# A block-recurrent attention and a mixture-of-depths layer on one core: another way out for the score rows, wider reads, and a new order

## The chip, the cores and the metric

The kernel runs on one core of a Trainium2 chip. The metric is the device time of one execution in microseconds. The core has five engines: PE (TensorE: matrix products and transposes, into PSUM), DVE (VectorE), ACT (ScalarE), POOL (GpSimd) and SP (SyncE, here only a queue that issues DMAs), and 16 DMA engines that all queues share.

## The reference, cut to what matters

```python
B, H, S, Ns, D = 8, 8, 512, 32, 64       # x: (B,H,S,D)   state: (B,H,Ns,D)
scores  = scale * x @ state^T;  a  = softmax(scores);   xread = a  @ state    # (B,H,S,D)
scores2 = scale * state @ x^T;  a2 = softmax(scores2);  sread = a2 @ x        # (B,H,Ns,D)
y = concat([xread, sread], axis=2)       # to (B, 544, 512): row s, column h*64 + d
scores = y @ w_gate                      # (B, 544)
for b in range(B):
    top = argpartition(-scores[b], 128)[:128]
    h   = maximum(y[b, top] @ w1, 0)     # w1: 512 x 1024
    out[b, top] = y[b, top] + sigmoid(scores[b, top]) * (h @ w2)   # w2: 1024 x 512; the other rows: out = y
```

All in float32.

## The kernel before, in words

The work is cut into some 690 named pieces, each on one engine. `add(name, engine, fn, after, takes, uses)` records a piece; `carry_out` then emits them in the sequence of the string `ORDER`, which is written out by hand: each engine runs its own pieces in that sequence and waits where it must. In a word such as `first3.4@6`, 3 is the batch, 4 a part of it, and 6 the PSUM bank that the piece takes; `~5@0` are five transposes of the identity that nobody uses. Eight batches overlap in this order. Per batch b:

- `ldx` loads x[b] (1 MB). `turn` transposes it on PE, four 128x128 transposes to a piece (L393), and `turned` copies the result out of PSUM on ACT (L402). For the batches in `ON_DVE` a second load `ldy` brings x in blocks, in 128-byte runs (L318), and `blocks` transposes 32x32 blocks on DVE (L382).
- `scores` (L418) gives both score matrices, heads four to a group g. `smax`, `sexp`, `ssum` are the softmax over the sequence; `xmax`, `xspread`, `xsub`, `xexp` are that over the state (batches 0 and 1 in halves).
- `read b.r` (L506) reads the state for half r of the rows. A head's 32 state rows lie on 32 partitions, four heads q beside each other; 16 matmuls of 32 x 128 by 66 columns: 64 of the state, one of gates (state times `w_gate`), one of ones. `zsum` inverts the sums, `gate` makes the row scores `sc[:, b, 2r:2r+2]`, `rows` scales the output rows (on ACT for chunks 1 and 3, else on DVE), `stx` stores them.
- `turna`/`turneda` transposes the second softmax on PE and ACT; for the batches in `A_BLOCKS`, `ablocks` turns blocks on DVE, and `aout` and four `ain` take them through DRAM (L544, L548). `sread` (L579) reads x, `srows` scales, `sts` stores.
- `sgate`, `heads`, `sscore`: gate of the state rows. A product with `w_gate` summed per partition, a matmul that adds up the heads, a copy of that column into `sc[:, b, 4]`.
- The scores must lie along the free dimension on all partitions (`srow`, 544 wide). Batches 0 to 3: `row b.r` and `srow` transpose the score columns on PE, `rowk` and `srowk` copy on ACT. Batches in `ROW_DMA`: `rowout` (four columns) and `srowout` (the state's) write them to DRAM element by element, `rowin` reads the row back broadcast to 128 partitions.
- `win` compares each score with all later ones, `over` adds up on PE, `off` and `oh` make a one-hot matrix of the chosen rows, `pick` on PE gives their numbers and scores. `fetch` (POOL, L611) gathers the 128 chosen rows from the stored output, so it waits for `stx` and `sts` too; `below`, `exps`, `sigmoid` make the gate.
- `xg` transposes the gathered rows (L770, copy `xgk`), `first b.0` to `first b.7` are the first layer (L792, eight records of 128 columns each), `relu` (L795), `second b.k.f0` the second (L814), `add` adds, `put` (POOL) scatters the rows.

A float32 matmul stands in the trace as two records. SP issues nearly all DMAs in the sequence of the order, so a DMA whose issue is held up holds up those behind it.

Of the kernel before, what the change touches and what calls it, by code (L numbers as in the profile page):

```python
# [8 lines left out]
F32 = mybir.dt.float32  # L9
# [22 lines left out]
    first0.0@1 sigmoid0 smax3 srowk1 xexp2 first0.1 ldw2.1 win1.0 sexp3.0 first0.2 xmax3 sexp3.1 first0.3 sexp2.1 xspread3
    first0.4@7 relu0.0 first0.5 ssum3 xsub3 turna2.1@6 first0.6 turneda2.1 ssum2 xexp3 ablocks3.0 read2.0@0 ablocks3.1 win1.1 aout3
    sread2@6 win1.2 stturn4@5 win1.3 srows2 ldy5.0 first0.7 win1.4 stkept4 sts2 sgate2 zsum2.0 over1@4 rows2.0 relu0.4 heads2
    second0.0.0@5 ain3.0 gate2.0 rows2.1 sscore2 off1 oh1 blocks4.0 second0.0.2 blocks4.1 ldy5.3 blocks4.2 ldy5.1 pick1 second0.0.4
    picked1 index1 below1 blocks4.3 fetch1 exps1 sigmoid1 read2.1@0 ldy5.2 second0.0.6 zsum2.1 rows2.2 rows2.3 gate2.1 ain3.1
    parts2 srow2 row2.0@7 add0.0 row2.1 rowk2 scores4.0@4 put0.0 srowk2 scores4.1 win2.0 stx2 xg1@7 smax4 read3.0@0 xgk1 blocks5.0
    sexp4.0 first1.0@7 zsum3.0 rows3.0 sexp4.1 first1.1 ain3.2 ablocks4.0 rows3.1 first1.2 ablocks4.1 first1.3 gate3.0 aout4 ssum4
    win2.1 row3.0@6 relu1.0 read3.1@0 win2.2 win2.3 first1.4@7 ain3.3 zsum3.1 gate3.1 rows3.3 rows3.2 first1.5 ain4.0 xmax4
    first1.6 xspread4 first1.7 stx3 sread3@3 relu1.4 xsub4 ain4.1 second1.0.0@7 xexp4 win2.4 ldx6.0 blocks5.1 ldx6.1 blocks5.2  # L40
    srows3 scores5.0@4 sts3 sgate3 blocks5.3 over2@2 scores5.1 off2 oh2 ain4.2 heads3 row3.1 pick2 smax5 second1.0.2 rowk3 index2
    sexp5.0 sscore3 fetch2 picked2 xmax5 second1.0.4 sexp5.1 ablocks5.0 below2 parts3 exps2 sigmoid2 second1.0.6 ain4.3 ablocks5.1
    ssum5 aout5 xspread5 srow3 xg2@6 srowk3 add1.0 read4.0@0 xgk2 xsub5 put1.0 sread4@7 zsum4.0 xexp5 ain5.0 gate4.0 first2.0@6
    rows4.0 ldy6.0 srows4 win3.0 first2.1 rows4.1 sgate4 first2.2 win3.1 sts4 win3.2 first2.3 ain5.1 win3.3 read4.1@0 win3.4
    relu2.0 ldx7.0 ldx7.1 over3@6 zsum4.1 heads4 gate4.1 rows4.3 first2.4@5 ldy6.1 sscore4 off3 parts4 oh3 first2.5 rows4.2
    first2.6 ain5.2 first2.7 second2.0.0@7 relu2.4 rowout4 pick3 read5.0@0 picked3 index3 ldy6.2 below3 fetch3 exps3 sigmoid3
    second2.0.2 ldy6.3 zsum5.0 rows5.0 gate5.0 rows5.1 second2.0.4 srowout4 ain5.3 second2.0.6 stx4 xg3@6 add2.0 rowin4 read5.1@0
# [12 lines left out]
    exps6 sigmoid6 second5.0.2 srows7 sts7 sgate7 heads7 second5.0.4 sscore7 parts7 srowout7 xg6@7 second5.0.6 rowin7 xgk6 add5.0  # L60
    first6.0@7 put5.0 first6.1 win7.0 first6.2 win7.1 first6.3 win7.2 win7.3 first6.4@6 relu6.0 win7.4 over7@7 first6.5 off7 oh7
# [8 lines left out]
def kernel(  # L70
# [10 lines left out]
    nc = tc.nc  # L81
# [172 lines left out]
    def pool_tables():  # L254
# [10 lines left out]
        for over in overs:  # L265
            nc.gpsimd.memset(over, 0.0)
# [621 lines left out]
```

## Time and profile before

| | |
|---|---|
| median of 3 runs (lowest, highest) | 251.94 us (251.03, 254.04) |
| the profiled execution | 251.55 us |
| its span, first to last instruction | 249.8 us |
| mean granted TensorE clock | 0.917 of full |
| busy: PE, weight loads, DVE, ACT, POOL | 202.0, 153.1, 121.2, 86.7, 34.8 us |
| DMA | 37.20 MB in 74945 packets, 61480 of them under 512 B |
| chain that ended last, by engine | DMA 32%, PE 26%, DVE 14%, ACT 10%, SP queue 8%, issue 7% |

Busy times are shares of one execution and add up over engines that work at the same time. The span is what the instructions take; the time of an execution is 1.75 us longer. The granted clock has two levels here, 1.00 for 2.4 GHz and 0.50 for 1.2.

### The profile page before, as it was taken

To read this page: it belongs to the slowest core of one execution; us is meant where nothing else is said; L and a number is where in the kernel's file an instruction comes from. 1 tells how busy PE (TensorE), PEld (TensorE's weight loads), DVE (VectorE), ACT (ScalarE), POOL (GpSimd) and SP (SyncE) were. 2 spreads that over 40 slices of the span, in tenths; PEclk is the share of its full clock that TensorE was granted. 3 is DMA by queue.
4 is the path that set the end of the run, shared out by engine and by line. 5 is a ranking of instruction groups with operands and counts; after the bars stand their busy time and mean duration, and the time that the engine had idled before them with its cause. 6 is when DMAs were issued, how large, how long until landed. Compare 5 with 4: busy or idle time off the path is not lost.

```text
span 249.8 us, 5630 instructions
## 1 busy us (share of the span) xinstructions
PE 202.0 (81%) x2305; PEld 153.1 (61%) x2305; DVE 121.2 (49%) x335; ACT 86.7 (35%) x257; POOL 34.8 (14%) x99
## 2 busy tenths in 40 slices
PE   7967896899799989992699959949249829889991
PEld 6646674795489439950579438925039624765981
DVE  3685686898386988331429507496104300240000
ACT  3675694865364236430033202072103101010000
POOL 8000203000220031121001201003100021120112
PEclk9997999999999999997569977999956968999999
DMA  7999989958965988799699592908429450600101
GB/s 211 330 339 356 253 275 207 251 201 149 173 210 151 285 181 146 211 82 69 132 220 80 117 169 106 129 2 269 27 76 106 40 175 11 89 10 31 45 0 42
DMA packets 74945, 37.20 MB, mean 149 GB/s; under 512 B 61480, under 2 KB 69672, under 8 KB 73896
## 3 DMA queue, kind: packets, MB, share of 16 engines
q1 hardware_dynamic: 72824, 32.26, 63.4%
q0 software_dynamic: 1296, 4.20, 7.2%
q8 instruction: 18, 0.29, 0.6%
q10 hardware_dynamic: 800, 0.39, 0.6%
q14 instruction: 7, 0.06, 0.1%
HBM read 23.20 MB, written 13.64 MB: 148 GB/s over the span
## 4 chain that ended last, share of the span: by engine, by line
DMA 32%; PE 26%; DVE 14%; ACT 10%; SPq 8%; issue 7%; POOLq 0%; POOL 0%; ACTq 0%; DVEq 0%
DMA xr<-out_dram,idx 12%; PE banks L792 7%; PE banks L814 6%; SPq L318 6%; ACT xs L524 6%; DMA xf<-in_x_dram 5%; DMA aT<-a_d 5%; PE banks L506 4%; DMA s_d<-sc 4%; DMA srow<-s_d 4%; PE banks L579 3%; DVE xs L526 2%; DVE nm L465 2%; PE banks L770 2%; DVE eT L456 2%
## 5 line engine op out<-in xcount | busy, mean ns | idle before, releaser
L792 PE MATMUL banks<-xg,w 128*128 128x128 f32 x512 | 65.9, 289 | 0.0
L792 PEld LDWEIGHTS banks<-xg,w 128*128 128x128 f32 x512 | 62.9, 203 | 2.7 <-issue 1.6
L814 PE MATMUL banks<-w,hT 128*128 128x512 f32 (+1 forms) x144 | 59.9, 559 | 3.2 <-ACT hT L795 3.2
L814 PEld LDWEIGHTS banks<-w,hT 128*128 128x128 f32 x144 | 26.3, 193 | 23.8 <-issue 19.4
L524 ACT ACTIVATE xs<-banks,rz 128x64 f32<-128x64 f32 x128 | 28.0, 332 | 22.6 <-DVE xs L526 12.2
L671 DVE SCALAR_TENSOR_TENSOR win<-srow,sc,after 128x544 bf16<-128x544 f32 (+4 forms) x40 | 18.3, 504 | 9.8 <-DMA srow<-s_d 9.2
L770 PE MATMUL banks<-ident,xr 128*128 128x128 f32 x32 | 6.4, 334 | 19.2 <-DMA xr<-out_dram,idx 19.2
L506 PEld LDWEIGHTS banks<-st_v,eT 32*128 32x128 f32 x512 | 19.2, 213 | 4.3 <-issue 3.2
L506 PE MATMUL banks<-st_v,eT 32*128 32x66 f32 x512 | 21.6, 305 | 0.2 <-ACT eT L460 0.2
L795 ACT ACTIVATE hT<-banks 128x512 f32<-128x512 f32 x16 | 9.7, 605 | 31.5 <-PE banks L792 31.1
L817 DVE SCALAR_TENSOR_TENSOR ot<-banks,z,xr 128x512 f32<-128x512 f32 (+1 forms) x9 | 6.1, 680 | 28.4 <-PE banks L814 28.4
L770 PEld LDWEIGHTS banks<-ident,xr 128*128 128x128 f32 x32 | 4.5, 170 | 23.6 <-issue 13.2
L382 DVE STREAM_TRANSPOSE xT<-xf 128x512 f32<-128x512 f32 x16 | 10.5, 688 | 17.4 <-DMA xf<-in_x_dram 17.4
L773 ACT COPY xg<-banks 128x512 f32<-128x512 f32 x8 | 4.7, 591 | 37.6 <-PE banks L770 37.6
L579 PE MATMUL banks<-xf,aT 128*32 128x64 f32 x512 | 11.3, 255 | 5.9 <-DMA aT<-a_d 5.5
L469 ACT ACTIVATE a<-banks,nm 128x512 f32<-128x512 f32 x16 | 11.1, 694 | 13.9 <-DVE nm L465 8.8
L579 PEld LDWEIGHTS banks<-xf,aT 128*32 128x32 f32 x512 | 9.8, 133 | 7.0 <-issue 6.5
L183 PE MATMUL banks<-ident 128*128 128x128 f32 x37 | 7.2, 346 | 7.8 <-ACT xs L524 3.2
L611 POOL DMA_INDIRECT xr<-out_dram,idx x8 | 8.4, 1047 | 34.3 <-DVE z L725 25.4
L526 DVE TENSOR_TENSOR xs<-banks,rz 128x512 f32<-128x512 f32 x16 | 10.9, 684 | 4.5 <-ACT xs L524 4.3
L418 PE MATMUL banks<-xT,st_T 64*32 64x256 f32 x256 | 12.2, 410 | 0.6 <-DVE eT L456 0.4
L611 POOL DMA_INDIRECT out_dram<-ot,idx x7 | 7.6, 1079 | 36.4 <-DVE ot L817 35.8
(87 smaller groups left out, 209.8 us busy)
## 6 DMA issues: line engine op xcount, KB each, us to landing
out_dram<-xs SPq DMA_DIRECT2D x8, 1024.0 KB
xf<-in_x_dram SPq DMA_DIRECT2D x14, 512.0 KB
xf<-in_x_dram SPq DMA_DIRECT2D x19, 256.0 KB
w<-in_moe_w_dram SPq DMA_DIRECT2D x4, 1024.0 KB
a_d<-a_b SPq DMA_DIRECT2D x5, 512.0 KB
aT<-a_d SPq DMA_DIRECT2D x20, 128.0 KB
srow<-s_d SPq DMA_DIRECT2D x4, 272.0 KB
out_dram<-xt SPq DMA_DIRECT2D x16, 32.0 KB
```

Of the source, the lines that this page charges most:

```text
L318: nc.sync.dma_start(out=view_x2(b)[o:o + 32], in_=src)
L418: nc.tensor.matmul(view_s()[Ns * q:Ns * (q + 1), w, g], st_T[half, b, g, Ns * q:Ns * (q + 1)], xT[2 * g + q // 2].ap[half, q % 2].rearrang ...
L469: nc.scalar.activation(out=a.ap[:, g], in_=view_s()[:, :, g], func=AF.Exp, bias=tmp["nm"][:, g:g + 1], accum_out=tmp["ss"][:, g:g + 1])
L506: nc.tensor.matmul(view(o)[:, q, w, g], eT.ap[k, w, g, r], st_v[k, b, g], start=True, stop=True)
L524: nc.scalar.activation(out=to[:, q, g], in_=view(o)[:, q, w, g, 0:D], func=AF.Copy, scale=rz[:, q, g:g + 1])
L526: nc.vector.tensor_tensor(out=to, in0=view(o)[:, :, w, :, 0:D], in1=rz.unsqueeze(3).to_broadcast([128, 4, 2, D]), op=ALU.mult)
L579: nc.tensor.matmul(o2.ap[k, D * g:D * (g + 1)], aT.ap[:, g, c, k], view_x(b)[:, 4 * g + q, c], start=(c == 0), stop=(c == NC - 1))
L611: touches(b, nc.gpsimd.indirect_dma_start(**kw), True)
L671: nc.vector.scalar_tensor_tensor(wins[c][0:n, 0:SP - f], srow.ap[0:n, f:SP], sc[0:n, b, c:c + 1], after[0:n, 0:SP - f], op0=ALU.is_gt, op1 ...
L770: nc.tensor.transpose(v[:, j, 0:m], u["xr"].ap[0:m, 128 * j:128 * (j + 1)], ident[0:m, 0:m])
L792: nc.tensor.matmul(o, w(j), i[:, :, j] if n == 256 else i[:, 0, j], start=(j == 0), stop=(j == ND - 1))
L814: nc.tensor.matmul(py.ap[0:m, 0:part.stop - part.start], hT.ap[:, f, lo:lo + m], w2[:, f, part], start=(f == 0), stop=(f == NF - 1))
```

## The change

- **Score rows through DRAM.** `sc` gets 32 columns per batch, zeroed at the start by POOL. A new DVE piece `rowblk` transposes its 32x32 blocks, so that each partition holds 32 scores in a row, and one DMA `rowout` writes 128 runs of 128 bytes, zero columns too (16 KB). `rowout`'s wait now includes the state's score; `srowout` is gone. `ROW_DMA` becomes batches 3 to 7.
- **Sums over heads.** `heads` multiplies the broadcast partial sums with `same_n`, 32 columns wide, which leaves the state's score row on all partitions at once; `srowk` copies it from there, `srow` is gone, and `sscore` takes the diagonal.
- **Wider reads.** For batches 1, 3, 5, 7 (`READ64`), POOL builds `st_2` (pieces `beside`): for each pair of heads the state of one in columns 0 to 65, of the other in 66 to 131, zeros elsewhere. A read is then 8 matmuls of 64 x 128 by 132 columns; `rows` on DVE takes two instructions instead of one. In all batches a PSUM bank now holds another part of the read.
- **Who turns what.** `ON_DVE` is 6 and 7 (was 4 to 7), `A_BLOCKS` 4 to 7 (was 3 to 7).
- **The order** is a new one. Ahead of `first0.0` now stand all turns of batches 0 to 5, the scores of 0 to 3, the state reads of 0 to 3 and the reads of x for 0, 1 and the first half of 2. Two stretches of it:

```text
(PE, from second2.0.0 to xg4)
second2.0.0@6 read4.0@0 over3@7 second2.0.2 pick3 second2.0.4 read4.1@0 second2.0.6 scores6.0@4 scores6.1 xg3@7 read5.0@0
first3.0@7 ... first3.7 read5.1@0 over4@7 second3.0.0@6 pick4 second3.0.2 sread5@7 scores7.0@4 scores7.1 read6.0@0 heads5
second3.0.4 xg4@7
(SP, in the same part)
ldy7.0 sts4 aout5 ldy7.3 ldy7.2 ain5.0 ldy7.1 ain5.1 rowout4 stx4 rowin4 ain5.2 aout6 ain5.3 ain6.0 ain6.1 stx5 ain6.2
```

```diff
-    ON_DVE = (4, 5, 6, 7) if planned else ()
-    A_BLOCKS = (3, 4, 5, 6, 7) if planned else ()
+    ON_DVE = (6,7)
+    A_BLOCKS = (4,5,6,7)
+    READ64 = (1,3,5,7)
-    ROW_DMA = (4, 5, 6, 7) if planned else ()
+    ROW_DMA = (3,4,5,6,7)
...
-    R_SD = Ring("s_d", [1, SP], 2, F32, dram)
+    R_SD = Ring("s_d", [32 * 128], 2, F32, dram)
+    R_SB = Ring("s_b", [128, 32], 2)
...
-    same_n = const.tile([128, 128], F32, name="same_n")
-    sc = const.tile([128, B, NC + 1], F32, name="sc")
+    same_n = const.tile([128, Ns], F32, name="same_n")
+    sc = const.tile([128, B, 32], F32, name="sc")
+    st_2 = const.tile([128, max(len(READ64), 1), 2, 2 * DV], F32, name="st_2")
...
+    def beside(b):
+        for q in range(4):
+            k, o = slice(Ns * q, Ns * (q + 1)), DV * (q % 2)
+            nc.gpsimd.tensor_copy(out=st_2[k, READ64.index(b), :, o:o + DV], in_=st_v[k, b])
+
+    for b in READ64:
+        p_bd[b] = add(f"beside{b}", "POOL", lambda b=b: beside(b), after=[p_sg[b], p_tab])
...
+                def read(r=r, o=o):
+                    for w in range(2):
+                        for g in range(2):
+                            for u in range(2):
+                                k = slice(2 * Ns * u, 2 * Ns * (u + 1))
+                                nc.tensor.matmul(view(o)[:, w, u, 2 * g:2 * g + 2].rearrange("p j m -> p (j m)"), eT.ap[k, w, g, r],
+                                                 st_2[k, READ64.index(b), g], start=True, stop=True)
...
         def sum_heads():
-            nc.tensor.matmul(o2.ap[:, 192:193], same_n, part[0], start=True, stop=True)
+            nc.tensor.matmul(o2.ap[:, 192:192 + Ns], part[0].to_broadcast([128, 128]), same_n, start=True, stop=True)
 
         def keep_state():
-            nc.vector.tensor_copy(out=sc[:, b, NC:NC + 1], in_=o2.ap[:, 192:193])
+            scr = small.tile([Ns, Ns], F32, name="scr2", bufs=1)
+            nc.vector.scalar_tensor_tensor(scr, o2.ap[0:Ns, 192:192 + Ns], 1.0, ident[0:Ns, 0:Ns], op0=ALU.mult, op1=ALU.mult,
+                                           accum_out=sc[0:Ns, b, NC:NC + 1])
...
-            def row_out(c0, c1):
-                n = Ns if c0 == NC else 128
-                nc.sync.dma_start(out=s_d.ap[0, 128 * c0:128 * (c1 - 1) + n].rearrange("(c p) -> p c", p=n), in_=sc[0:n, b, c0:c1])
+            def row_blocks():
+                nc.vector.transpose(out=s_b.ap, in_=sc[:, b])
+
+            def row_out():
+                nc.sync.dma_start(out=s_d.ap.rearrange("(c q t) -> q c t", q=4, t=32), in_=s_b.ap)
...
-            p = [add(f"rowout{b}", "SP", lambda: row_out(0, NC), after=p_sc, takes=[s_d])]
-            p.append(add(f"srowout{b}", "SP", lambda: row_out(NC, NC + 1), after=[p_ss, p[0]], uses=[s_d]))
-            p_r1 = p_r2 = add(f"rowin{b}", "SP", row_in, after=p, takes=[srow], uses=[s_d])
+            p = add(f"rowblk{b}", "DVE", row_blocks, after=p_sc + [p_ss], takes=[s_b])
+            p = add(f"rowout{b}", "SP", row_out, after=[p], takes=[s_d], uses=[s_b])
+            p_r1 = p_r2 = add(f"rowin{b}", "SP", row_in, after=[p], takes=[srow], uses=[s_d])
...
-            p = add(f"srow{b}", "PE", row_s, after=[p_ss], uses=[o2])
-            p_r2 = add(f"srowk{b}", "ACT", lambda: nc.scalar.copy(out=srow.ap[:, S:SP], in_=o2.ap[:, 256:256 + Ns]), after=[p, p_r1],
+            p_r2 = add(f"srowk{b}", "ACT", lambda: nc.scalar.copy(out=srow.ap[:, S:SP], in_=o2.ap[:, 192:192 + Ns]), after=[p_hd, p_r1],
                        uses=[srow, o2])
```

## Rows read from the trace of the kernel before

**Rows 1.** Busy time by stretch, the stretches cut where the PE starts the transposes of the next batch's chosen rows (`xg0` at 45.0 us, `xg1` at 69.5, and so on to `xg7` at 228.3); the last line is the sum. Columns: the stretch and its length, then busy us and (instructions) of PE, weight load, DVE, ACT and POOL, the granted clock of TensorE as a share of 2.4 GHz, the mean busy share of the 16 DMA engines, and GB/s moved.

```profile
0.00:45.00 45.00, 34.54 (x519) 27.29 (x520) 28.94 (x75) 28.76 (x79) 9.03 (x34) 0.96 1.00 283
45.00:69.50 24.50, 23.10 (x313) 16.75 (x311) 18.09 (x48) 13.89 (x40) 2.25 (x8) 1.00 0.90 192
69.50:93.50 24.00, 22.62 (x278) 15.47 (x272) 19.99 (x49) 10.62 (x33) 3.46 (x9) 1.00 0.76 201
93.50:120.90 27.40, 20.12 (x266) 15.29 (x267) 10.49 (x37) 8.81 (x31) 4.98 (x11) 0.91 0.94 133
120.90:147.10 26.20, 22.92 (x235) 16.81 (x236) 13.75 (x36) 6.65 (x19) 2.19 (x7) 0.83 0.92 140
147.10:184.60 37.50, 25.72 (x299) 19.19 (x299) 17.90 (x48) 9.93 (x35) 4.51 (x11) 0.86 0.58 111
184.60:211.00 26.40, 20.89 (x199) 16.63 (x200) 5.73 (x24) 4.25 (x14) 2.19 (x7) 0.75 0.61 81
211.00:228.30 17.30, 15.73 (x105) 11.41 (x104) 4.55 (x17) 1.98 (x4) 2.82 (x7) 1.00 0.29 47
228.30:249.80 21.50, 16.39 (x105) 14.24 (x103) 1.72 (x3) 1.78 (x3) 3.37 (x6) 0.98 0.07 25
sum 249.80, PE 202.01 PEld 153.07 DVE 121.16 ACT 86.68 POOL 34.78; mean PE 22.45 PEld 17.01 DVE 13.46 ACT 9.63 POOL 3.87
```

**Rows 2.** Timeline of PE: the five places where it stands longest behind 46 us. Columns: start, us, engine, line, operation, tiles, shapes, count, and in brackets the idle time before with what ended it.

```profile
120.90 1.09 PE L770 MATMUL banks<-ident,xr 128*128 128x128 f32 x4 [7.26 <-DMA xr<-out_dram,idx]
...
147.06 1.09 PE L770 MATMUL banks<-ident,xr 128*128 128x128 f32 x4 [2.92 <-DMA xr<-out_dram,idx]
...
165.66 1.98 PE L814 MATMUL banks<-w,hT 128*128 128x512 f32 x4 [3.24 <-ACT hT L795]
...
184.58 1.12 PE L770 MATMUL banks<-ident,xr 128*128 128x128 f32 x4 [8.21 <-DMA xr<-out_dram,idx]
...
204.43 1.94 PE L579 MATMUL banks<-xf,aT 128*32 128x64 f32 x64 [5.51 <-DMA aT<-a_d]
```

**Rows 3.** Timeline of the SP queue: DMA issues, with start and the time that the issue held the queue. L641 is the way out of the score columns (`rowout` first, then `srowout`), L606 the state rows of the output (two DMAs of 32 KB each).

```profile
106.51 0.61 SPq L641 DMA_DIRECT2D s_d<-sc  x1
...
110.21 9.94 SPq L641 DMA_DIRECT2D s_d<-sc  x1
...
130.88 0.38 SPq L641 DMA_DIRECT2D s_d<-sc  x1
...
170.66 0.44 SPq L641 DMA_DIRECT2D s_d<-sc  x1
...
189.30 0.62 SPq L641 DMA_DIRECT2D s_d<-sc  x1
...
206.76 1.24 SPq L606 DMA_DIRECT2D out_dram<-xt  x2
```

**Rows 4.** Busy time by stretch again, for four stretches that each begin 1.5 to 3.7 us behind one of the issues of `rowout`, and for the two us in which the state rows of the last batch go out with nothing else queued. Columns as in Rows 1.

```profile
108.00:117.00 9.00, 5.64 (x24) 2.35 (x20) 2.43 (x8) 1.75 (x8) 2.29 (x4) 0.94 1.08 49
132.50:141.00 8.50, 8.50 (x67) 6.32 (x67) 7.73 (x24) 2.84 (x7) 2.19 (x7) 1.00 1.05 62
174.00:182.00 8.00, 2.37 (x6) 0.76 (x4) 0.95 (x2) 1.75 (x8) 1.72 (x5) 0.93 0.47 34
193.00:200.00 7.00, 5.92 (x57) 4.76 (x55) 2.67 (x12) 1.19 (x2) 0.18 (x1) 1.00 0.44 37
...
208.00:210.00 2.00, 2.00 (x7) 0.98 (x6) 0.16 (x1) 0.00 (x0) 0.35 (x2) 0.96 0.15 33
```

**Rows 5.** The chain of work that ended last: start, us, what. Four of its pieces that are DMAs, each counted from its issue to its landing.

```profile
108.33 12.44 DMA xr<-out_dram,idx
...
171.59 12.95 DMA xr<-out_dram,idx
...
192.17 12.01 DMA aT<-a_d
...
209.52 3.04 DMA s_d<-sc
```

**Rows 6.** Busy time by stretch for the four stretches with the lower clock behind the gaps of Rows 2. Columns as in Rows 1.

```profile
120.90:129.30 8.40, 8.03 (x132) 6.66 (x140) 3.79 (x9) 1.61 (x7) 0.00 (x0) 0.50 0.73 179
147.10:153.20 6.10, 6.10 (x51) 5.65 (x52) 2.35 (x4) 0.59 (x1) 0.13 (x1) 0.50 0.86 135
184.60:191.10 6.50, 6.50 (x52) 6.05 (x53) 1.47 (x5) 2.34 (x9) 0.00 (x0) 0.50 0.26 47
204.40:208.10 3.70, 3.67 (x66) 2.56 (x67) 0.30 (x2) 0.52 (x2) 0.00 (x0) 0.50 0.02 5
```

**Rows 7.** Prices. From the timeline of PE (start, us, what): one read of x as it is now (32 records), and the 64 records of a whole first layer. From the groups by line and shape (busy us, mean ns of one | idle before): the copy that ends a transpose of x on PE, the transpose of x on DVE, a small copy on POOL. Last, from the view of the tile `xr`: us from issue to landing of its gathers, at least, median, at most.

```profile
94.08 1.12 PE L506 MATMUL banks<-st_v,eT 32*128 32x66 f32 x32
...
230.47 7.31 PE L792 MATMUL banks<-xg,w 128*128 128x128 f32 x64
...
L382 DVE STREAM_TRANSPOSE xT<-xf 128x512 f32<-128x512 f32 x16 | 10.5, 688 | 17.4 <-DMA xf<-in_x_dram 17.4
...
L402 ACT COPY xT<-banks 128x512 f32<-128x512 f32 x15 | 8.5, 595 | 2.1 <-PE banks L393 2.0
...
L684 POOL CAST aux<-rest 128x5 bf16<-128x5 f32 x8 | 2.1, 262 | 0.5
...
DMA to landing us min/median/max: 3.3/5.9/12.9
```

More of the change, by code (lines that the diff above doesn't have):

```diff
@@ L44 @@
[L44 to L47, printed above, removed]
@@ new lines @@
+    rowin3 xg2@7 add1.0 scores5.0@2 xgk2 put1.0 scores5.1 sread4@7 smax5 first2.0@6 ldy7.0 srows4 xmax5 sexp5.0 sts4 first2.1
+    sexp5.1 ablocks5.0 first2.2 ablocks5.1 first2.3 ssum5 aout5 xspread5 first2.4@5 relu2.0 first2.5 xsub5 ldy7.3 first2.6 ldy7.2
+    sgate4 xexp5 win3.0 first2.7 win3.1 heads4 second2.0.0@6 relu2.4 sscore4 win3.2 ain5.0 win3.3 win3.4 read4.0@0 over3@7 zsum4.0
+    ldy7.1 second2.0.2 off3 oh3 rows4.0 pick3 gate4.0 rows4.1 second2.0.4 index3 picked3 fetch3 ain5.1 read4.1@0 below3 exps3
@@ new lines @@
+    sigmoid3 second2.0.6 zsum4.1 gate4.1 rows4.3 rowblk4 parts4 rows4.2 rowout4 scores6.0@4 add2.0 scores6.1 stx4 blocks7.0 put2.0
+    rowin4 xg3@7 smax6 read5.0@0 xgk3 ain5.2 first3.0@7 xmax6 sexp6.0 sexp6.1 first3.1 ablocks6.0 first3.2 ablocks6.1 xspread6
+    aout6 first3.3 first3.4@6 relu3.0 zsum5.0 gate5.0 first3.5 rows5.0 ain5.3 win4.0 first3.6 rows5.1 ain6.0 win4.1 first3.7 win4.2
+    read5.1@0 relu3.4 win4.3 win4.4 xsub6 over4@7 second3.0.0@6 off4 ain6.1 xexp6 oh4 pick4 zsum5.1 second3.0.2 rows5.2 rows5.3
@@ L110 @@
     planned = cap == 128
[L111 to L112 removed]
+    ON_DVE = (6,7)
+    A_BLOCKS = (4,5,6,7)
     HALVED = (0, 1)
[L114 to L115 removed]
+    READ64 = (1,3,5,7)
+    ROW_DMA = (3,4,5,6,7)
+    ACT_ROWS = tuple((b, c) for b in range(B) for c in (1, 3))
     GROUPS = [[0],[1],[2],[3],[4],[5],[6],[7]]
@@ L207 @@
     R_XR = Ring("xr", [128, Dm], 6)
-    R_XG = Ring("xg", [128, 2, ND, 128], 2 if planned else 1)
-    R_HT = Ring("hT", [128, NF, 256], 1)
+    NG = max(len(g) for g in GROUPS) if planned else 2
+    R_XG = Ring("xg", [128, NG, ND, 128], 2 if planned else 1)
+    R_HT = Ring("hT", [128, NF, 128 * NG], 1)
     R_IDX = Ring("idx", [128, 1], 8, I32)
@@ L511, in sums @@
+                nc.vector.tensor_scalar_add(t, v, 1e-9)
                 nc.vector.reciprocal(out=rz, in_=rz)
             def gate(r=r, o=o):
[L514 to L526 removed]
@@ L528, in attention @@
-            p = add(f"read{b}.{r}", "PE", read, after=[p_eT[r], p_sg[b], p_tab] + p_sc, takes=[o] if r else [o, xs], uses=[eT])
+                t = small.tile([128, 2, 2, 4], F32, name="gt")
+                rz = tmp["rz", r]
+                if b in READ64:
+                    nc.vector.tensor_tensor(out=t.rearrange("p w u j -> p (w u) j"), in0=view(o)[:, :, :, :, D].rearrange("p w u j -> p (w u) j"),
+                                            in1=rz.rearrange("p w u j -> p (w u) j"), op=ALU.mult)
+                else:
+                    nc.vector.tensor_tensor(out=t.rearrange("p w u (k g) -> p w (u k) g", g=2), in0=view(o)[:, :, :, :, D],
+                                            in1=rz.rearrange("p w u (k g) -> p w (u k) g", g=2), op=ALU.mult)
@@ L529, in attention @@
+                nc.vector.reduce_sum(out=sc[:, b, 2 * r:2 * r + 2], in_=t.rearrange("p w u j -> p w (u j)"), axis=AX.X)
+            p = add(f"read{b}.{r}", "PE", read, after=[p_eT[r], p_bd.get(b, p_sg[b]), p_tab] + p_sc, takes=[o] if r else [o, xs], uses=[eT])
             p = add(f"zsum{b}.{r}", "DVE", sums, after=[p], uses=[o])
```

156 lines of the change are left out of this document (82 added, 74 removed).

## The prediction

> **What bounds the kernel now.** I read the views in this order: busy time by stretch, PE's own waits, the DMA throughput in the stretches around those waits, the SP queue, and the chain that ended last.
>
> The stretches [rows 1] run from one batch's chosen rows to the next (xg to xg), so each holds one batch's two layers and whatever attention work the order puts beside them. PE is busy 202.0 of 249.8 us, and in the second and third stretch 23.1 of 24.5 and 22.6 of 24.0: there PE is the bound and little is left. From the fourth on it is not: 20.1 of 27.4, 22.9 of 26.2, 25.7 of 37.5, 20.9 of 26.4. Nearly all of that is five waits [rows 2]: 7.26 + 2.92 + 3.24 + 8.21 + 5.51 = 27.1 us. Four of them are ended by a DMA, the 3.24 by ACT, which hangs on a late score row.
>
> After four of the gaps the granted clock stands at 0.50, 1.2 instead of 2.4 GHz [rows 6]. PE's busy time in these stretches is 8.03 + 6.10 + 6.50 + 3.67 = 24.3 us, half of which, 12.15, is the price of the clock. Together the gaps take 39.3 us.
>
> What they share stands in [rows 3, 4]. `rowout` writes the scores of a batch to DRAM as 512 single elements of 4 bytes. It is issued at 106.5, 130.9, 170.7 and 189.3 us, and 1.5 to 3.7 us behind each issue a stretch of 7 to 9 us begins in which the 16 DMA engines move 34 to 62 GB/s, where the first five stretches average 133 to 283 [rows 1]. Whatever was issued around it lands late: two gathers of chosen rows take 12.4 and 12.95 us [rows 5] against 3.3 at best and 5.9 in the median [rows 7], one quarter of aT takes 12.0, and the issue of `srowout` holds the SP queue 9.94 us [rows 3]. That these writes are the cause is an inference: four issues, four slow stretches, each followed by one of the gaps. DMA's large share of the chain is then mostly the price of four small transfers.
>
> **The change, part by part.** Base: the gaps of [rows 2] and the clock behind them taken out of the span, 249.8 - 27.1 - 12.15 = 210.5 us.
>
> *Score rows.* One DVE block transpose and one DMA of 128 runs of 128 bytes take the place of `rowout` and `srowout`, for five batches instead of four. The trace has no DRAM write in 128-byte runs. The nearest rows are the state rows, 128 runs of 256 bytes per DMA: with nothing else queued two are issued at 206.76 [rows 3], and in 208 to 210 us 33 GB/s pass, 66 KB, at a busy share of 0.15 [rows 4]: both are through in under 2 us. From the other side, 512 writes hold the engines 8 us on average over the four stretches, 0.016 us each; 128 such writes would be 2 us. I take 0 to 2 us of slow DMA per batch, which the PE work hides, and count the removal as the whole 39.3. A landing stays: 32 elements with idle queues took 3.04 us [rows 5], so from a batch's last gate to its row I keep about 3 us plus the broadcast read. The row-out is now one DMA that waits for the state's score as well (sread, srows, sgate, heads, sscore, rowblk); behind it on SP stand stx, rowin and the next `ain` pieces, and who waits is win, over, pick. In the new order some 13 us of PE work stand between read4.1 and over4 (a whole first layer of 7.31 us [rows 7], two reads of 1.12, a quarter of a second layer, two scores, a transpose group), so this wait is covered. Bounds of the block transpose: nothing to one DVE transpose of 688 ns [rows 7].
>
> The Trainium skill, "DMA: Bandwidth & Descriptors", Specifications, wants at least 512 bytes per transfer and says that anything smaller is read-modified-written, so 128-byte runs are still on the wrong side. By that rule the stall would shrink with the count of writes, not vanish; the 256-byte state rows, also under 512, show no stall here.
>
> *Sums over heads.* heads keeps its one matmul, now 32 columns wide, and gives the row already spread over the partitions; srow (a wait for sscore and a transpose, four batches) goes. sscore, a copy of one column, becomes a 32x32 product with a diagonal: nothing to the 0.69 us of a large DVE operation [rows 7], in stretches where DVE is under 83% busy [rows 1]. I count zero; uncovered it would be at most 8 x 0.69 = 5.5 us.
>
> *Batches 4 and 5 turn x on PE.* Out: 8 DVE transposes of 688 ns [rows 7] and two loads of 1 MB in 128-byte runs. In: 8 groups of four PE transposes and 8 ACT copies of 595 ns [rows 7]. Batch 3 turns its `a` on PE: two more groups and copies in, 512 KB out and back through DRAM gone. Four transposes take 1.09 us at the half clock [rows 2], so 0.55 at the full, 0.137 each. Counting both orders: 40 added for x and a, 8 gone from row and srow, 13 fillers gone: 19 x 0.137 = +2.6 us of PE.
>
> *Two heads side by side.* For batches 1, 3, 5, 7 a read is 16 records of 132 columns in two halves of the array instead of 32 records of 66 in four quarters. Now: 1.12 us [rows 7], 0.035 per record. A first-layer record of 128 columns takes 7.31 / 64 = 0.114 [rows 7]; 16 of 132 columns are 1.88 us in series, 0.94 if the halves overlap. So -0.2 to +0.76 us per read, -1.4 to +6.1 for eight. I take +0.3 each, +2.4: today's records overlap about three to one, so I expect the halves to overlap too. On POOL 16 copies (262 ns for a short one [rows 7], so 4 us, 8 if twice as long) lie in a stretch where POOL is busy 9 of 45 us [rows 1]; `read` of batch 1 waits for the first four, due long before.
>
> *The new order.* By the pieces of both orders, each priced by its rows, the work before xg0 grows by 7 us on PE, 11 on ACT and 7 on DVE: all turns of batches 3, 4 and 5 move there, with batch 3's scores and reads of `a`. From busy times of 34.5, 28.8 and 28.9 of 45 us [rows 1] these come to about 42, 40 and 36. The 7 us on PE are only moved, so what counts is idle time: 10.5 us now, and three engines nearly equally full; I take +3.5, bounds 0 and +10 (xg0 at about 56 us). Later, pick3 to xg3 holds only two pieces of the second layer, a read and two scores, some 6 us of PE work, beside the load of batch 7 in 128-byte runs: the gather takes 5.9 or more there, so I add 3 us of gap and clock for this one.
>
> Sum: 210.5 + 2.6 + 2.4 + 3.5 + 3 = 222.0 us of span. The profiled execution took 251.55 for a span of 249.8, so +1.75: 223.8. It stands 0.4 under the median of the runs, 251.94. I say 223.
>
> **The rivals.** *The small writes still stall the engines.* Four stalls cost 39.3 us, 9.8 each; five at that price put 49 us on 223.8, 273: slower. It decides if a stall still costs over 27.7 / 5 = 5.5 us. For it: the runs are still short, and the first two gathers behind them are covered no better than now; against it, the state rows of [rows 4]. Chance 0.07.
>
> The Trainium skill, "DMA: Bandwidth & Descriptors", "Why a DMA increments its semaphore by 16 and not by 1", has an engine count that divides the slowest dimension of both sides; the new DRAM side begins with 4, so four engines would write 32 runs each, as many as each of sixteen writes now. No row here shows the engine of a packet.
>
> *The start fills up.* ACT carries 40 us of work before xg0; if idle time there grows by 10 and the wide reads don't overlap: 223.8 + 6.5 + 3.7 = 234. For it: in today's start neither engine is above 77% [rows 1]. Chance 0.2.
>
> *The gathers stay late without the 4-byte writes.* If 128-byte loads and 1 MB stores are enough for 12 us, xg3 and xg4 each wait some 5 to 6 us, with 2 to 3 us of clock behind: 223.8 + 16 = 240. For it: the wait of 2.92; against it, 5.9 as the median in a queue that is 58 to 100% busy [rows 1]. Chance 0.13.
>
> **How the numbers follow.** The forecast has 0.6. Its own ends: 210.5 + 2.6 - 1.4 = 211.7 of span, 213.5 in all, and some us less if the order also saves small waits; upward 234. The range 210 to 240 takes in the second and third rival and leaves out the first. A measurement of this kernel can tell about 1%, 2.5 us. Faster by more: all but the first rival and some mixtures of the other two, 0.88; within 1%: 0.04; slower: 0.08.
>
> **What would show it.** Right: no stretch under 70 GB/s behind the run-outs, gathers landing in under 7 us, no PE gap over 4 us behind xg0, the clock at 1.00 from there on, xg0 between 52 and 60 us, PE busy near 195. Wrong: gathers of 10 us or more behind a run-out (first rival), xg0 behind 62 us or reads of 1.8 us (second), gaps at xg3 and xg4 with loads of x in 128-byte runs queued (third).

## The result, and the profile after

The changed kernel takes 210.64 us (median of 4 runs, 210.6 to 211.51), the kernel before 252.99 in the same session: a ratio of 0.836, 95% interval 0.829 to 0.843. Two later sessions gave 0.850 (0.837 to 0.862) and 0.848 (0.843 to 0.852). So it is faster by 15 to 16%, 0.6 us above the lower end of the forecast range; the forecast of 223 was 12 us too high.

First the chain that ended last in the changed kernel, from its page. The kernel before had DMA in front with 32%.

```profile
span 208.8 us, 5427 instructions
...
PE 191.8 (92%) x2196; PEld 146.6 (70%) x2196; DVE 117.4 (56%) x345; ACT 90.3 (43%) x265; POOL 40.2 (19%) x117
...
PE 69%; DVE 11%; ACT 9%; issue 7%; DMA 1%; POOLq 1%; POOL 0%; DVEq 0%; ACTq 0%
```

PE now carries the chain, DMA 1% of it. Where the time went is seen in the busy time by stretch, cut at xg0 to xg7 as in [rows 1], same columns.

```profile
0.00:55.40 55.40, 45.47 (x713) 36.33 (x713) 37.98 (x94) 40.44 (x104) 14.23 (x52) 0.88 0.78 266
55.40:70.75 15.35, 14.99 (x168) 11.97 (x165) 7.93 (x33) 7.54 (x28) 2.14 (x7) 1.00 0.91 230
70.75:92.30 21.55, 21.55 (x149) 15.09 (x148) 13.52 (x40) 7.68 (x25) 3.39 (x9) 1.00 0.32 87
92.30:113.60 21.30, 21.30 (x299) 14.98 (x297) 13.46 (x40) 8.49 (x27) 3.29 (x9) 1.00 0.77 167
113.60:135.65 22.05, 20.36 (x270) 15.21 (x263) 20.25 (x56) 11.30 (x39) 3.37 (x9) 1.00 0.67 190
135.65:154.50 18.85, 18.84 (x218) 14.31 (x219) 11.55 (x38) 7.10 (x24) 3.26 (x9) 1.00 0.61 161
154.50:172.30 17.80, 17.80 (x187) 13.30 (x186) 8.86 (x38) 4.24 (x14) 3.89 (x9) 1.00 0.39 133
172.30:182.30 10.00, 10.00 (x94) 8.93 (x93) 2.18 (x7) 1.27 (x3) 3.28 (x7) 1.00 0.16 52
182.30:208.80 26.50, 21.50 (x118) 16.52 (x116) 1.72 (x3) 2.27 (x4) 3.33 (x6) 0.95 0.05 20
sum 208.80, PE 191.81 PEld 146.64 DVE 117.45 ACT 90.33 POOL 40.19; mean PE 21.31 PEld 16.29 DVE 13.05 ACT 10.04 POOL 4.47
```

Read PE's busy time against the length of each stretch. From xg1 to xg7 PE stands still 1.70 us in all (the differences of the six stretches), at a granted clock of 1.00; in [rows 1] the same way from xg1 to xg7 left 30.8 idle and the clock at 0.75 to 1.00. The first stretch has the lowest clock, 0.88; the 0.95 of the last one comes from its end, where PE has nothing left to do (1.00 from 182.3 to 203.8 us, and no PE work behind).

The score rows, in the timeline of the SP queue (start, us that the issue held the queue): `rowout` is L693, `rowin`, which waits for it, L696.

```profile
90.22 0.57 SPq L693 DMA_DIRECT2D s_d<-s_b  x1
92.27 0.32 SPq L696 DMA_DIRECT2D srow<-s_d  x1
112.03 0.56 SPq L693 DMA_DIRECT2D s_d<-s_b  x1
114.53 0.42 SPq L696 DMA_DIRECT2D srow<-s_d  x1
...
164.47 0.52 SPq L693 DMA_DIRECT2D s_d<-s_b  x1
166.40 0.33 SPq L696 DMA_DIRECT2D srow<-s_d  x1
```

From issue to the next issue pass 1.9 to 2.5 us here (3.6 and 2.9 in the other two batches), where the issue of `srowout` alone was held 9.94 in [rows 3]. Three stretches by busy time: the second row-out of the five between its two issues, and ten us around the first and the second row-out (columns as in [rows 1]):

```profile
112.00:114.50 2.50, 2.50 (x42) 1.22 (x42) 1.08 (x3) 1.59 (x8) 0.63 (x4) 1.00 0.04 7
...
88.00:98.00 10.00, 10.00 (x137) 6.65 (x136) 4.87 (x10) 4.08 (x15) 1.98 (x6) 1.00 0.67 173
110.00:120.00 10.00, 10.00 (x126) 7.87 (x123) 7.03 (x15) 4.38 (x14) 1.98 (x6) 1.00 0.61 180
```

While the new write goes out with almost nothing else queued, the busy share of the 16 DMA engines is 0.04; behind the old ones it was 0.44 to 1.08, with 34 to 62 GB/s passing [rows 4]. The view of the tile `xr` gives the gathers, issue to landing, against 3.3/5.9/12.9 in [rows 7]:

```profile
DMA to landing us min/median/max: 3.3/3.5/6.8
```

And the only wait of PE over 0.35 us behind xg0, in its timeline, is at xg4 (second row from the same kernel, profiled again in a later session):

```profile
135.66 0.63 PE L818 MATMUL banks<-ident,xr 128*128 128x128 f32 x4 [1.58 <-DVE a_b L588]
```

```profile
136.49 0.63 PE L818 MATMUL banks<-ident,xr 128*128 128x128 f32 x4 [0.58 <-DMA xr<-out_dram,idx]
```

The first row names DVE, but `xg` waits for `fetch` and takes nothing from `ablocks`. The gather of this batch, issued at 128.76, is the one that takes 6.8 us, so it lands at 135.5, together with the end of the DVE work; in the second row, and in a third trace with 0.68 us, the gather itself is named. The slow DMA of [rows 4] is not seen there: from 128.7 to 135.6 us the DMA engines move 222 GB/s at a busy share of 0.75. `stx5`, a store of 1 MB, is issued right behind the gather at 128.91; that it makes the gather late is argued, not shown.

Of the five gaps of [rows 2], four are gone, and the one at xg4 has shrunk from 2.92 to 0.6 to 1.6 us, with no lower clock behind it.

### The profile page after: what moved, and what is told of

Same layout as the page of the kernel before. It is cut to its first block, busy times and chain, and to the rows that moved or that the text cites. A ratio compares the mean times of both kernels' runs of the same rounds, so it can differ in the third digit from the quotient of the medians.

```text
span 208.8 us, 5427 instructions
## 1 busy us (share of the span) xinstructions
PE 191.8 (92%) x2196; PEld 146.6 (70%) x2196; DVE 117.4 (56%) x345; ACT 90.3 (43%) x265; POOL 40.2 (19%) x117
## 4 chain that ended last, share of the span: by engine, by line
PE 69%; DVE 11%; ACT 9%; issue 7%; DMA 1%; POOLq 1%; POOL 0%; DVEq 0%; ACTq 0%
PE banks L840 21%; PE banks L862 21%; PE banks L546 5%; PE banks L627 5%; PE banks L523 4%; PE banks L433 3%; PE banks L408 3%; ACT xs L554 3%; ACT a L484 2%; ACT xT L417 2%; PE banks L183 2%; PE banks L818 2%; PE banks L743 1%; DVE a_b L588 1%; DVE mx L456 1%
## 5 line engine op out<-in xcount | busy, mean ns | idle before, releaser
L840 PE MATMUL banks<-xg,w 128*128 128x128 f32 x512 | 61.4, 278 | 0.0
L532 ACT ACTIVATE xs<-banks,rz 128x64 f32<-128x64 f32 x64 | 14.0, 333 | 10.5 <-DVE rz L563 8.8
L417 ACT COPY xT<-banks 128x512 f32<-128x512 f32 x23 | 13.3, 598 | 3.6 <-PE banks L408 3.2
L408 PE MATMUL banks<-ident,xf 128*128 128x128 f32 x96 | 13.8, 286 | 1.1 <-ACT xT L417 0.7
L546 PEld LDWEIGHTS banks<-st_v,eT 32*128 32x128 f32 x256 | 9.0, 203 | 6.7 <-issue 5.4
L408 PEld LDWEIGHTS banks<-ident,xf 128*128 128x128 f32 x96 | 10.6, 144 | 4.3 <-ACT xT L417 1.1
L546 PE MATMUL banks<-st_v,eT 32*128 32x66 f32 x256 | 10.3, 295 | 3.3 <-DVE eT L471 3.2
L475 ACT ACTIVATE eT<-eT 128x1024 f32<-128x1024 f32 (+1 forms) x10 | 9.0, 905 | 7.2 <-DVE eT L471 7.2
L480 DVE TENSOR_REDUCE nm<-banks 128x2 f32<-128x1024 f32 x8 | 9.7, 1219 | 3.6 <-PE banks L433 3.6
L471 DVE TENSOR_TENSOR eT<-banks,eT 128x1024 f32<-128x1024 f32 (+1 forms) x10 | 10.1, 1008 | 1.3 <-ACT a L484 1.0
L523 PEld LDWEIGHTS banks<-st,eT 64*128 64x128 f32 x128 | 9.0, 204 | 2.5 <-issue 1.7
```

What stands on the lines that cost most here:

```text
L408: nc.tensor.transpose(v[:, k, r], view_x(b)[:, 2 * pair + k, 2 * r:2 * r + 2].rearrange("p w d -> p (w d)"), ident)
L417: nc.scalar.copy(out=t.ap, in_=v)
L523: nc.tensor.matmul(view(o)[:, w, u, 2 * g:2 * g + 2].rearrange("p j m -> p (j m)"), eT.ap[k, w, g, r], st_2[k, READ64.index(b), g], start= ...
L532: nc.scalar.activation(out=to[:, u, j // 2, j % 2], in_=view(o)[:, w, u, j, 0:D], func=AF.Copy, scale=rz[:, u, j:j + 1])
L546: nc.tensor.matmul(view(o)[:, w, q, g], eT.ap[k, w, g, r], st_v[k, b, g], start=True, stop=True)
L840: nc.tensor.matmul(o, w(j), i[:, :, j] if n == 256 else i[:, 0, j], start=(j == 0), stop=(j == ND - 1))
```

## The experiments

**One part alone: the form of the write.** The old order and everything else of the kernel before; only batches 4 to 7 write their score rows in 128-byte runs.

```diff
- rowout4 ... srowout4                 # ORDER, batches 4 to 7
+ rowblk4 rowout4
- nc.sync.dma_start(out=s_d.ap[0, 128*c0:128*(c1-1)+n].rearrange("(c p) -> p c", p=n), in_=sc[0:n, b, c0:c1])
+ nc.vector.transpose(out=s_b.ap, in_=sc[:, b])
+ nc.sync.dma_start(out=s_d.ap.rearrange("(c q t) -> q c t", q=4, t=32), in_=s_b.ap)
```

> The kernel before with one part of the change alone: the score row of batches 4 to 7 goes to DRAM in 128 runs of 128 bytes (block transpose, one write behind the state's score) instead of 512 + 32 single elements; order, reads and loads as before. If the 4-byte writes cause the four gaps and the cold clock behind them, 39.3 us go: 251.6 - 39 = 212 us, between 207 and 222, and no stretch behind a write of scores moves under 70 GB/s. If instead the loads of x in 128-byte runs, or the old order, hold up the DMA engines, the gaps stay and it takes 240 us or more.

208.67 us (208.07 to 209.6), ratio 0.838 (0.831 to 0.845). The whole gain, from this edit alone. The sum and the gathers of its profile, and the longest wait of PE behind xg0, which is for DVE; no xg waits for its gather:

```profile
sum 207.80, PE 187.87 PEld 142.86 DVE 121.96 ACT 86.60 POOL 34.85; mean PE 20.87 PEld 15.87 DVE 13.55 ACT 9.62 POOL 3.87
...
DMA to landing us min/median/max: 3.3/3.9/6.7
...
68.33 0.43 PE L658 MATMUL banks<-ident,sc 128*128 128x128 f32 x2 [1.40 <-DVE sc L518]
```

The base of the prediction's sum was 210.5 us, of it 189.9 of PE at full clock; here it stands by itself: 207.8 and 187.9.

**The reverse: everything but the form of the write.** The changed kernel, with rows written as single elements again.

```diff
- nc.sync.dma_start(out=s_d.ap.rearrange("(c q t) -> q c t", q=4, t=32), in_=s_b.ap)
+ for c0, c1, n in ((0, NC, 128), (NC, NC + 1, Ns)):
+     nc.sync.dma_start(out=s_d.ap[128*c0:128*(c1-1)+n].rearrange("(c p) -> p c", p=n), in_=sc[0:n, b, c0:c1])
```

> The changed kernel with one part taken back: the score rows of batches 3 to 7 go to DRAM as single elements again (512 of 4 bytes and 32 of 4 bytes, from the score columns), all else as changed; the block transpose on DVE stays. If the 4-byte writes are the cause, five stalls return at 5 to 10 us each: 235 to 260 us, with gathers of 10 us and more behind them. If the new order and the dropped loads removed the gaps, it stays under 222 us.

240.87 us (240.74 to 242.3), ratio 0.970 (0.961 to 0.978). Five rows bring back 30.3 us of span (239.1 against 208.8), 6.1 each. PE's waits, longest first (PE line, released by: us in total, times, longest us), the first row out and in on SP, and ten us around the first and the second row-out, as shown for the changed kernel above:

```profile
PE banks L627 <- DMA aT<-a_d: 7.1, 2, 5.5
PE banks L744 <- DVE win L720: 6.0, 5, 5.0
PE banks L627 <- issue: 5.7, 1, 5.7
PE banks L819 <- DMA xr<-out_dram,idx: 3.9, 2, 2.5
...
90.91 0.93 SPq L694 DMA_DIRECT2D s_d<-sc  x2
101.50 0.32 SPq L697 DMA_DIRECT2D srow<-s_d  x1
...
90.00:100.00 10.00, 5.44 (x75) 2.62 (x74) 3.69 (x6) 1.02 (x4) 1.99 (x6) 0.88 0.92 59
119.00:129.00 10.00, 10.00 (x105) 7.93 (x106) 7.52 (x13) 4.38 (x14) 1.99 (x6) 1.00 0.76 58
```

The first experiment also moved the write to a later place, behind the state's score; here the single elements go out at that same place, so it is the form of the write that counts and not its time. The slow DMA is back: 59 and 58 GB/s at busy shares of 0.92 and 0.76, where the changed kernel moved 173 and 180 (116, 72 and 18 against 228, 107 and 92 around the other three). The kinds of waits of [rows 2] are back too: quarters of aT, a gather, and the row itself (`win`). The gathers are not as late as expected: the longest takes 7.5 us, not 10. The row needs 10.6 us instead of 2.0. The third wait is new: in the middle of the group of 64 records of L627 PE pauses from 95.4 to 101.17 us with no releaser in the trace, until the row is out (its way in is issued at 101.50). The page lists a DMA queue of kind "instruction", but late instructions do not fit: none of its packets begins between 84.2 and 103.1 us, and PE goes on at 101.17. What held PE stays open.

**The price of a write by itself.** Three kernels are the changed one with small writes from SBUF to DRAM behind the last `rowin`, where SP has nothing to do, each followed by a read-back that waits for it.

> The changed kernel with seven extra writes to scratch DRAM at the end of the SP queue, where it is empty, each followed by a read-back that waits for its landing, so that the distance from the issue of a write to the issue of its read-back is its price. In this order: 128 runs of 128 bytes as the changed kernel writes them; 512 single elements side by side in DRAM, as before; 512 single elements 128 bytes apart; 512 runs of 32 bytes; 128 single elements; 128 runs of 256 bytes; 128 runs of 128 bytes in partition order. If single elements are slow because neighbours share a stretch of DRAM: about 2, 8 to 10, 2 to 3, 3 to 5, 2 to 4, 2, 2 us. If each small write costs the same whatever its place and length: about 2 to 4, 8 to 10, 8 to 10, 8 to 10, 3 to 4, 2 to 4, 2 to 4. If the 512 elements are not slow with an empty queue, the second is 2 to 4 like the others, and the stall needs other traffic.

> The changed kernel with nine writes to DRAM behind the last row read, each followed by a small read back that waits for it. Theory: single elements that are neighbours in DRAM are written one after the other, some 0.05 us each within 512 bytes, and 512-byte stretches go in parallel. From issue of write to issue of read back, with 1.4 us for a write by itself: 128 x 64 B side by side 2, 32 singles 3, 64 singles 4.5, 256 singles 7 to 8, 128 singles 16 B apart 3, 64 B apart 1.8, 512 B apart 1.4 to 2, 128 x 16 B side by side 3, 128 singles 7. Rival A, the number of descriptors counts: all with 128 alike at 7, 32 singles 2, 256 singles 8. Rival B, the stretch is 64 bytes: 32 and 64 singles 7 as 128, 16 B apart 3, 64 B apart 1.5.

> The changed kernel with eight writes and read-backs behind the last row read; the last four are the question and lie where POOL issues no gather or scatter: 64 single elements side by side, 128 at a pitch of 8 bytes, 48 side by side, 32 side by side. In the run before, 32 took 2.97 us and 64 took 7.75 with a scatter and a gather beside them, 128 7.15, 256 7.85. If the price is one element after the other, 64 alone take 4 to 5 and 48 3.5 to 4; if there is a step, 64 take 7 to 8 again and 48 either 3 or 7. 128 at 8 bytes lie between 2.74 (16 bytes) and 7.15 (4 bytes).

Some rows of SP's timeline, of the second and the third of these kernels; each pair is a write and its read-back:

```profile
171.47 0.31 SPq L918 DMA_DIRECT2D pd<-sc  x1
174.44 0.22 SPq L919 DMA_DIRECT2D back<-pd  x1
...
182.72 0.39 SPq L918 DMA_DIRECT2D pd<-sc  x1
190.57 0.23 SPq L919 DMA_DIRECT2D back<-pd  x1
...
197.92 0.34 SPq L918 DMA_DIRECT2D pd<-sc  x1
199.33 0.23 SPq L919 DMA_DIRECT2D back<-pd  x1
```

```profile
177.88 0.51 SPq L917 DMA_DIRECT2D pd<-sc  x1
186.30 0.23 SPq L918 DMA_DIRECT2D back<-pd  x1
186.59 0.34 SPq L917 DMA_DIRECT2D pd<-sc  x1
189.54 0.23 SPq L918 DMA_DIRECT2D back<-pd  x1
189.82 0.30 SPq L917 DMA_DIRECT2D pd<-sc  x1
194.97 0.22 SPq L918 DMA_DIRECT2D back<-pd  x1
```

The first three pairs are 32 single elements side by side, 256 of them, and 128 pieces of 16 bytes; the last three 64 singles, 128 singles at a pitch of 8 bytes, 48 singles. All of them, from issue to issue (a star: a gather or scatter of POOL was issued meanwhile or up to 1.5 us before; the starred prices are not those of the write by itself):

| write | us |
|---|---|
| 128 pieces side by side of 16, 128, 256 bytes | 1.41, 1.42 and 1.43*, 1.46 (256 bytes also 3.56*) |
| 128 pieces of 128 bytes, as the changed kernel places them; of 64 bytes | 2.69*; 2.85* |
| 512 pieces of 32 bytes side by side | 1.78 |
| 512 singles 128 bytes apart | 2.30, 3.41*, 3.72* |
| 128 singles 512, 64, 16, 8 bytes apart | 1.42, 2.10*, 2.74*, 2.95 |
| singles side by side: 32, 48, 64 | 2.97 and 2.98*, 5.15, 7.75* and 8.42* |
| singles side by side: 128, 256, 512 | 7.01* and 7.15*, 7.85, 8.48* |

It is not the number of pieces: 512 pieces of 32 bytes, and 512 singles spread out, are through in 1.78 and 2.30 us. It is not smallness alone either: 128 singles take 1.42 when 512 bytes apart. Slow are 4-byte elements that lie next to one another: without a star 48 take 5.15 and 256 take 7.85. The 64 were meant to be measured alone, but a gather was issued 1.5 us behind them; beside POOL's transfers they are as slow as 512. The 128 singles already missed in the first of the three kernels, where 2 to 4 us were expected. All three rules laid down before the second one fall: one element after the other at 0.05 us gave 3 for the 16-byte pieces (1.41) and 4.5 for 64 singles (7.75), the count alone gave one price for all with 128 pieces, the stretch of 64 bytes gave 7 for 32 singles (2.97). In the third, 48 singles fit neither a steady price (3.5 to 4) nor a step (3 or 7). Between 32 and 64 singles the price climbs from 3 to 8 us and then stays; why is open.

The Trainium skill, "DMA: Bandwidth & Descriptors", Specifications, says that below 512 bytes a transfer is read-modified-written; all these pieces are below it and most are quick, so here the rule does not tell which write stalls. Whether the count of engines from its section "Why a DMA increments its semaphore by 16 and not by 1" matters is not shown: the 2.69 for the changed kernel's placement had a gather beside it, and so had the 2.85. In the changed kernel itself this write takes 1.93 us where no gather is near (164.47 to 166.40), so its placement costs some 0.5 us over the 1.42 at most.

What happens beside such a write is seen in the second and the third kernel. In the third, the gather of the last batch was issued at 179.35, 1.5 us behind the 64 singles (first row: PE's timeline at xg7). In the second, POOL's last scatter waited for the one before, which ran beside the 128 singles (second row: POOL's timeline).

```profile
186.59 0.63 PE L818 MATMUL banks<-ident,xr 128*128 128x128 f32 x4 [2.81 <-DMA xr<-out_dram,idx]
```

```profile
209.69 0.96 POOL L659 DMA_INDIRECT out_dram<-ot,half  x1 [5.18 <-DMA out_dram<-ot,half]
```

Beside 256 bytes a gather took 7.1 us to landing, the longest of its run, where the same gather of the changed kernel takes 3.3; then PE waited 2.81, and its clock fell behind the wait: the 16 second-layer records took 8.73 us where the changed kernel needs 7.03. Beside 512 bytes a scatter took 5.5 us where the next one, with no such write beside it, takes 2.4. The three kernels, run once each, took 209.82, 215.41 and 216.61 us.

**All reads narrow.** The changed kernel with `READ64 = ()` and without the `beside` pieces.

> The changed kernel with all sixteen reads in the old form, 16 matmuls of 32 x 128 by 66 columns, and without the POOL copies that the wide form needs; all else as changed. A wide read stands in the trace with 1.10 us from start to start against 1.06 for a narrow one, so the theory that the wide form neither costs nor gives expects 210.6 us within 1.0. If the wide reads gave part of the gain (other banks, fewer records), it is slower by 2 us or more; if they cost the 0.3 us each of the prediction, faster by 2 us or more.

215.09 us (214.84 to 215.37), ratio 0.865 (0.858 to 0.871): 4.5 us slower than the changed kernel's 210.64, a miss. The two were not run beside each other, and the old order with long runs differs by 4.0 us between two chips (208.67 and 212.65), so how much of the 4.5 is due to the reads is not shown. xg0 comes 2.6 us later, and the stretches from xg3 to xg6 are 2.1 us longer. The first of these, and PE at two places in it:

```profile
115.92:138.56 22.64, 21.70 (x303) 16.18 (x296) 18.61 (x48) 9.74 (x31) 3.38 (x9) 0.92 0.66 184
...
125.90 1.72 PE L545 MATMUL banks<-st_v,eT 32*128 32x66 f32 x32 [0.94 <-ACT xs L553]
...
127.94 2.87 PE L861 MATMUL banks<-w,hT 128*128 128x512 f32 x4
```

PE waits 0.94 us for `rows` on ACT to empty the bank, and the read then takes 1.72 us for 1.12, still at a clock of 1.00. The clock falls later: it stands at 0.50 from 128.86 to 132.27 us, and four second-layer records take 2.87 us for 1.96. In the start, PE waits 1.53 instead of 0.99 us for the same ACT work, and pauses 1.04 and 1.40 us in the middle of two reads without a releaser in the trace; but such a pause, 1.39 us, stands in the second trace of the changed kernel too. The records themselves differ by next to nothing (timeline of PE in the changed kernel, a wide and a narrow read):

```profile
77.83 1.17 PE L523 MATMUL banks<-st,eT 64*128 64x132 f32 x16
...
104.35 1.12 PE L546 MATMUL banks<-st_v,eT 32*128 32x66 f32 x32
```

**Wide reads in the old order.** The first experiment, plus wide reads for batches 3, 5 and 7.

```diff
+ READ64 = (3, 5, 7)
+ beside3 behind stgate2, beside5 beside7 behind stgate4    # ORDER
```

> The old order with 128-byte runs, and with two heads side by side in the reads of batches 3, 5 and 7 (six reads of 16 records in place of 32), nothing else of the change. Theory (a wide read costs PE 1.17 against 1.12 us, and DVE two operations of 417 ns for one of 690): six times 0.05 on PE, 0.14 on DVE for each of its rows; 208.7 to 209.5 us. By the price in the prediction, 0.3 each, 210.5. Rival: the wide reads are a gain by themselves, as the narrow ones in the new order cost 4.5 us: 205 to 207.

209.68 us (208.94 to 210.4), ratio 0.843 (0.832 to 0.854), against 0.838 and 0.851 for the old order without them: no difference that shows. So wide reads give no measurable gain by themselves; that what the narrow ones cost above belongs to an order written around the wide ones is argued, not shown.

**Holding the clock in the start.** The changed kernel with 18 products that nobody uses in the two bubbles of the start.

```diff
- read0.0@0 ... row0.1
+ %10@5 read0.0@0 ... ^8@6 row0.1     # 10 matmuls of ident, 8 transposes of ident
```

> The changed kernel with 10 matmuls into an unused part of a bank ahead of read0.0 and 8 transposes ahead of row0.1, in the two bubbles of the start (3.19 us ahead of 21.80, 2.23 ahead of 33.91) behind which its clock is halved for some 11 us. Theory: the 5.5 us that PE loses to the half clock before 40 us are on the path; the fillers (18 x 0.06 to 0.14 us) keep the clock at 1.00 and xg0 comes 2 to 4 us sooner: 207 to 209 us against 210.6. Rival: the start is set by ACT and DVE (40.4 and 38.0 busy of 55.4 us), PE's half clock is hidden beside them, and nothing moves: 210.6 within 1.

> The changed kernel itself on the chip of the two others, to compare them with it: 210.6 us, 0.836 of the kernel before. Against the old order with 128-byte runs alone (0.838 before) the theory has no difference over 1%.

211.86 us (211.1 to 212.57) with them, 211.43 (210.56 to 212.9) for the changed kernel on the same chip. Busy time up to xg0, with the fillers and without:

```profile
0.00:54.96 54.96, 46.11 (x741) 37.39 (x741) 38.37 (x99) 41.20 (x106) 14.34 (x52) 0.97 0.82 274
```

```profile
0.00:55.72 55.72, 44.03 (x712) 35.05 (x713) 37.98 (x94) 40.32 (x104) 14.24 (x52) 0.91 0.78 265
```

The clock is held, 0.97 for 0.91, and xg0 hardly moves: there PE is not what sets the time, and a slow clock is hidden in its idle time. The fillers last 4.31 us, so PE's real work in the start is some 41.8 us.

**The two orders side by side.** Old order with 128-byte runs, and the changed kernel, five rounds on one chip.

> The old order with 128-byte runs alone, beside the changed kernel on one chip. So far 208.7 us (0.838 of before) on one chip, and the changed kernel 210.6 and 211.4 (0.836 and 0.850). Theory: all that the change brings is the form of the write, the rest cancels: the two within 1%, the old order 0 to 2.5 us shorter, since it has some 2 us less PE work at full clock and the same idle time. Rival: the new order is worth something once the stalls are gone: the changed kernel shorter by 1 us or more.

> The changed kernel beside the old order with 128-byte runs: theory 210.6 to 211.5 us, 0 to 2.5 us over the other; rival 1 us or more under it.

212.65 us (211.38 to 215.48), ratio 0.851 (0.844 to 0.858), against 211.81 (211.15 to 212.09), ratio 0.848 (0.843 to 0.852). The same, within the intervals; the 0 to 2.5 us that the old order was expected to be shorter do not show. Neither order beats the other once the single elements are gone; with them, the new order was worth 9 us (240.87 against 249.87).

## Why the prediction was right, and where its size was off

**Right: the mechanism.** That the single-element writes cause all five gaps and the half clocks behind them was an inference from four issues and four slow stretches. It holds both ways: taken out alone, 41 us go (249.87 to 208.67; predicted 39.3 of span), all five gaps with them; put back alone, 30 us come, and the DMA engines move 59 and 58 GB/s for 173 and 180. The first rival, that short runs still stall, needed 5.5 us a row; single elements cost 6.1 each in the new order, 128-byte runs nothing that PE sees. The argument that decided it, the state rows in 256-byte runs through in 2 us, was the right row. The price of 0.016 us per element behind the upper bound was a wrong picture: 512 singles spread out take 2.30 us, 256 side by side 7.85, so the stall hangs on neighbours and not on the number alone.

**Off: what the rest of the change costs.** The sum said 210.5 + 11.5 = 222.0 of span; the page says 208.8.

- *The start, +3.5*: right. xg0 was put at about 56 us, it came at 55.4. PE's work there is 41.8 (priced 42), ACT's 40.4 (40), DVE's 38.0 (36), and idle time, in the run with the fillers and its clock of 0.97, 54.96 - 41.8 = 13.2 us instead of 10.5: +2.7.
- Nearly all of the error lies behind xg0: 153.4 us, where the sum left 166. Half of it is PE work: 146.3 us against 189.9 + 5.0 - 42 = 152.9. Of these 6.6, 2.0 were in the base (the first experiment has 187.9 for 189.9), and 2.0 are the wide reads: eight at +0.05, not +0.3. The two halves of the array overlap about as the four quarters do: 1.88 us in series, by the prediction's price per column, against 1.17 and 1.12 measured, 1.6 and 1.7 to one. (The "three to one" of the prediction set a record of 66 columns against one of 128.) The rest is the term for transposes and fillers: 41.8 + 146.3 = 188.1 is all of PE's work, so the whole change adds 0.2 us to the 187.9, not 5.0, and this term came out at -0.2 for +2.6. The fillers were priced too low as savings: by the groups of the first experiment and of the changed kernel 13 fewer save 2.7 us (7.4 to 4.7), 0.2 each and not 0.137. That is 0.9 of the 2.8; no row tells where the rest went.
- The other half is idle time, 7.1 us behind xg0 against 20.7 - 10.5 + 3 = 13.2. The 3 us for a late gather at xg3 did not come: it was issued at 108.34 and PE did not wait at 113.61; the load of batch 7 had been issued by 104. A late gather came one batch later, at xg4, and cost 1.58 us. The other 3 us are small waits of the kernel before, which the base kept and which went too.

**The second and third rival.** The second fell: xg0 at 55.4 and no read of 1.8 us at full clock. The third is there in small: at xg4 a gather beside a store of 1 MB takes 6.8 us, not 12, and PE waits 0.6 to 1.6 us in three traces of the changed kernel, not 5 to 6, with the clock at 1.00 behind it. Each term of the sum that had no direct row was put above zero, and the wide reads, the transposes and the gather at xg3 all came out at about nothing. The forecast's own lower end, 211.7 of span, was still 3 us too high: it named the small waits that a new order can also save, without putting a number to them, though the 20.7 us of idle time that the base kept were there to be read. That 210.64 still lies in the range, whose end of 210 stands 3.5 us under that lower end of 213.5, is luck: no row carried those 3.5 us.

## What to carry to other kernels

Look for DMAs that write single 4-byte elements to neighbouring addresses in DRAM, even if they are only some hundred bytes (32 singles cost 3 us here, 48 cost 5): their price is paid by whatever other transfer is in flight, a gather, a load, and by PE's clock behind it. Turn the block on chip first, so that each partition writes a run (16 bytes were enough by themselves here, 128 in the kernel). When a row names what ended a wait, look also at what else landed at that moment: at xg4 it was the gather. And when one cause stands in several gaps, try its removal alone before the rest of the plan: here the new order, the wider reads and the other turns were worth nothing measurable once it was gone.

## What the runs showed of the hardware that was not expected

- 256 single elements side by side in DRAM take 7.85 us, 48 take 5.15 (64, with a gather and a scatter beside them, 7.8 to 8.4); 128 of them 512 bytes apart take 1.42, 128 pieces of 16 bytes side by side 1.41, 512 pieces of 32 bytes 1.78.
- Beside such a write a gather lands after 7.1 us instead of 3.3 and a scatter after 5.5 instead of 2.4, on another queue.
- Once PE paused 5.7 us in the middle of a group of matmuls, with no releaser in the trace and no packet of an instruction queue in that time, and went on as such a write was done.
- Behind a wait of 0.94 us and a slow read at a clock of 1.00, the clock stood at 0.50 from 128.86 to 132.27 us, 3 us behind that wait; behind one of 1.58 us in another run it did not fall (the stretch behind 135.65 has 1.00).
